# New order lists for the first eight steps of a fused attention and two-MoE kernel, with quotients, weight shifts, casts and low parts of g given out engine by engine

## The chip, the core and the metric

The kernel runs on one core of one Trainium2 chip. The metric is device microseconds of one launch. The kernel before has a median of 916.74 us over 3 runs (916.73 to 917.19).

## The reference

A banded attention feeds two feed-forward layers, all in fp32 to the reader; the weights come as 8-byte numbers.

```
scores = q k^T / 8, kept where 0 <= row - column < 64      4 batches, 8 heads, 576 rows, head size 64
x = softmax(scores) v                                      x: 2304 tokens x 512
g = x w_gate;  silu = g / (1 + exp(-g));  x = (silu * (x w_val)) w_out      inner size 1536
h = x w2_in;   out = max(0.01 h, h) w2_out                                  inner size 2048
```

## The kernel before, in words

The tokens are cut into five blocks. Block 0 holds 512 tokens and is worked in two halves of 256 (batch 0 and batch 1); blocks 1 to 4 hold 448 each. Per block the program first needs its attention, then the first layer in steps. One step takes 128 columns of the inner size: 12 matmuls for the gate (G), 12 for the value (W), 12 into the four output accumulators (O). Block 0 takes 24 steps, the others 12 each. The second layer follows, as products of halves in the manner of Strassen. Every matmul of the layers is done three times, with a high and a low part of both operands.

A weight piece of 128 x 512 comes in by a DMA (D) into one of three buffers `raw`. Five instructions make it ready: U on ScalarE scales the high word into `u` (L319), A shifts the low word right by 29 (L321), B joins the two (L323), C casts `u` to the high part (L330), E subtracts for the low part (L331). The buffer is free for the next DMA but two once B has read it. Each step has three pieces: g, v and o.

The attention of block 0 is eight jobs, 0 to 3 for the first half, 4 to 7 for the second, two heads each. A job n is: N, four transposes of q and k on TensorE; K, their eviction (L210); S, its scores; M and X, mask with row maximum and exponential, per tile t of 128 x 128; R, two small instructions for the reciprocals of the sums; Q, the quotient of a tile (L255); T, its transpose (L263); P, the eviction of T (L268); V, the values (L281); H and L, the high and low part of x (L291, L292). G of the first half needs H and L of jobs 0 to 3, quarter c of its matmuls those of job c. Per step also follow th, y (on G's result), z (on W's), gh and gl, the high and low part of the activation (L652, L654, L664, L666, L667). O needs gl.

Which instruction stands where on an engine comes from priorities, except at the start: `ORDER` names the instructions of the first steps engine by engine, and every instruction in such a list is tied behind the one before it. Each engine runs its own list strictly in order, so one that waits holds all behind it. In the kernel before all 32 quotients of block 0 are on GpSimd, all A on VectorE, all C on ScalarE and all gl on GpSimd; the lists end with G6, W6 and O5. Behind them the attention of block 1 (jobs 8 to 15) is laid into the remaining steps of block 0 by due times: job 8's are counted from slot 29, three slots to a step. Its q and k are turned by three transposes on VectorE (L214, L217).

Of the kernel before, what the change touches and what calls it, by code (L numbers as in the profile page):

```python
# [8 lines left out]
F32 = mybir.dt.float32  # L9
# [4 lines left out]
P = 128  # L14
# [13 lines left out]
def banded_attention_moe_moe(  # L28
# [99 lines left out]

    xt = {}
# [28 lines left out]
    class Job:  # L158


        def __init__(self, n, blk, xoff, b, u0, T, hp, first):
            self.n, self.blk, self.xoff, self.b, self.T, self.hp = n, blk, xoff, b, T, hp
            self.early = blk == 0
            self.half = u0 > 0
            self.N = 64 * T
# [77 lines left out]
        def norm(self, i, engines):  # L243
# [5 lines left out]
            for t, engine in zip(ts, engines):  # L249
                if engine is nc.scalar:  # L250
                    turn = nc.scalar.activation(e[:, t], e[:, t], AF.Copy, scale=st[:, 3, t:t + 1])
                elif engine is nc.vector:
# [4 lines left out]
                note(f"Q{self.n}.{t}", turn)  # L257

        def transpose(self, i):
            ts = self.fills[i]  # L260
            ps = (ps_acc if self.n < 4 else ps_att).tile([P, 4, P], F32, tag=self.bank, name="pt")
            for a, t in enumerate(ts):
                turned = note(f"T{self.n}", nc.tensor.transpose(ps[:, a], self.e[:, t], ident))  # L263
                if not self.early:
                    in_turn(turned)
            soon()
            note(f"P{self.n}",
                 nc.scalar.copy(self.pT[:, self.tile0 + ts[0]:self.tile0 + ts[-1] + 1], ps[:, :len(ts)]))  # L268
# [34 lines left out]
    def fetch(src, gated=False, key=None):  # L303
# [4 lines left out]
        note(key and "D" + key,  # L308
# [3 lines left out]
    def narrow(raw, gated=False, key=None):  # L312
# [16 lines left out]
    def split(hi, lo, u, key=None):  # L329
        note(key and "C" + key, nc.scalar.copy(hi, u))  # L330
        note(key and "E" + key, nc.vector.tensor_tensor(lo, u, f32(hi), op=ALU.subtract))  # L331

    def fetch1(f, c, gated=False):
        cs, cs2 = slice(f * P, f * P + P), slice(f * 2 * P, f * 2 * P + 2 * P)
        src = {"g": w_gate, "v": w_val, "o": w_out}[c]
        return fetch(src[cs, :] if c == "o" else src[:, cs2].rearrange("(c p) f -> p c f", p=P), gated, c + str(f))

    def convert1(f, c, raw, gated=False):
        u = narrow(raw, gated, c + str(f))
# [3 lines left out]
        split(w[:, 0], w[:, 1], u, c + str(f))  # L343
# [186 lines left out]
    for _ in range(8):  # L530
# [4 lines left out]
        (-0.61, "N0 N1 S0 S1 N3 N2 S3 S2 T0 T1 V0 T2 V1 T3 V2 V3 N6 N5"),  # L535
        (0.39, "N7 N4"),
        (2.39, "S7 S4"),
        (3.39, "S5 S6"),
        (5.39, "T7 T4"),
        (6.39, "V7 V4"),  # L540
        (7.39, "T5"),
        (8.39, "T6 V5"),
        (9.39, "V6"),
    )

    def early(part, j):
# [8 lines left out]
        elif part == "T":  # L555
            j.norm(0, [nc.gpsimd] * 4)
            j.transpose(0)
# [10 lines left out]

    for slot, parts in EARLY:
        for part in parts.split():  # L570
            at(slot, lambda part=part: early(part[0], jobs[int(part[1:])]))

    for n, j in enumerate(jobs):
# [67 lines left out]
    def step1(slot, blk, cols, f, first, last, behind=lambda *a: None, key=None):  # L641
# [25 lines left out]
        note(f"gl{key}", nc.gpsimd.tensor_tensor(g[1][:, :n], th, f32(g[0][:, :n]), op=ALU.subtract))  # L667
# [31 lines left out]
    for i, (part, f) in enumerate(order):  # L699
# [5 lines left out]
        for f1 in range(HELD, NF1):  # L705
# [7 lines left out]

    ORDER = {
        "tensor":
            "N0 N1 S0 S1 N3 N2 S3 S2 T0 T1 V0 T2 V1 T3 V2 V3 N6 N5 G0 N7 N4 W0 S7 S4 G1 S5 S6 W1 O0 T7 T4 G2 V7 "
            "V4 W2 T5 O1 T6 V5 G3 V6 W3 O2 G4 W4 O3 G5 W5 O4 G6 W6 O5",
        "vector":
# [5 lines left out]
        "scalar":  # L724
# [333 lines left out]
```

## Time and profile before

| | us |
|---|---|
| median of 3 runs | 916.74 |
| the profiled execution, its own time | 916.74 |
| its span, from the first to the last instruction | 914.9 |
| TensorE busy in the span | 900.2 |
| granted TensorE clock, mean | 0.998 |

The first slice of the profile's 40 shows TensorE at 7 tenths, the last at 8, all others at 9; so what TensorE leaves empty is to be looked for at the start and the end. VectorE is at 9 tenths in slices 2 and 5 of the start. The DMA engines' mean share is 9, 7, 6, 7 tenths in the first four slices.

### The profile page before, as it was taken

The page shows a single profiled execution, that of the slowest core. Times are in us where ns is not written, and L with a number is a line of the kernel's source. Part 1 is how long each engine was busy: PE and PEld are TensorE (multiplying, and loading weights), DVE is VectorE, ACT ScalarE, POOL GpSimd, SP SyncE. Part 2 cuts the span into 40 slices and gives each one's busy share as a digit, 9 for nine tenths or more (in the row PEclk, how much of TensorE's full clock was granted, in tenths as well). Part 3 has the DMA queues.
Part 4 walks back from the last instruction along what each step waited for, and adds up shares of the span by engine and source line. Part 5 has one row for each costly group of instructions (what it writes and reads, how often), then busy time and mean ns, then how long its engine had stood idle before and what let it go on. Part 6 is the DMA issues. An engine that isn't in the chain of part 4 may idle for free.

```text
span 914.9 us, 18179 instructions
## 1 busy us (share of the span) xinstructions
PE 900.2 (98%) x6147; PEld 855.6 (94%) x6147; DVE 661.3 (72%) x1525; ACT 462.3 (51%) x1153; POOL 374.3 (41%) x541
## 2 busy tenths in 40 slices
PE   7999999999999999999999999999999999999998
PEld 6899999899899999999999999999999999999997
DVE  5988974465666666566445546899998899978787
ACT  6956664554555545546433325544536445454442
POOL 4433321112212212212222135666666666675555
PEclk9999999999999999999999999999999999999999
DMA  9767642446576566746543966876568783588842
GB/s 232 214 176 201 189 119 48 114 152 200 163 207 170 170 177 189 210 144 212 171 178 136 338 208 208 266 236 222 176 196 286 243 255 114 164 281 264 247 152 81
DMA packets 198524, 176.32 MB, mean 193 GB/s; under 512 B 118048, under 2 KB 146976, under 8 KB 198432
## 3 DMA queue, kind: packets, MB, share of 16 engines
q1 hardware_dynamic: 196288, 174.64, 62.7%
q8 instruction: 49, 0.80, 0.4%
q10 hardware_dynamic: 2144, 0.52, 0.3%
q14 instruction: 43, 0.35, 0.1%
HBM read 135.27 MB, written 39.85 MB: 191 GB/s over the span
## 4 chain that ended last, share of the span: by engine, by line
PE 81%; DVE 7%; DMA 4%; POOL 2%; issue 2%; ACT 2%; SPq 1%; DVEq 0%; POOLq 0%; ACTq 0%
PE pv L610 14%; PE acc L610 14%; PE pg L610 14%; PE y L826 12%; PE px L783 7%; PE pw L783 5%; PE py L783 5%; PE yc L826 5%; PE s L227 2%; DMA raw<-in_moe_w_val_dram 2%; DVE space L820 2%; PE pv L281 1%; PE pt L263 1%; POOL g L805 1%; DVE u L323 1%
## 5 line engine op out<-in xcount | busy, mean ns | idle before, releaser
L667 POOL TENSOR_TENSOR g<-th,g 128x448 fp32r<-128x448 f32 (+1 forms) x72 | 82.0, 1138 | 265.0 <-ACT g L666 253.4
L610 PE MATMUL pv<-x,w 128*128 128x448 f32 (+1 forms) x864 | 172.0, 344 | 0.4 <-DVE w L331 0.2
L610 PE MATMUL pg<-x,w 128*128 128x448 f32 (+1 forms) x864 | 168.8, 342 | 1.7 <-DVE th L654 1.0
L610 PE MATMUL acc<-g,w 128*128 128x448 f32 (+1 forms) x864 | 166.0, 340 | 0.0
L610 PEld LDWEIGHTS acc<-g,w 128*128 128x128 f32 x864 | 144.4, 189 | 9.3 <-POOL g L667 0.3
L610 PEld LDWEIGHTS pg<-x,w 128*128 128x128 f32 x864 | 142.7, 189 | 10.8 <-DVE th L654 1.2
L610 PEld LDWEIGHTS pv<-x,w 128*128 128x128 f32 x864 | 142.2, 189 | 10.8 <-issue 0.7
L826 PE MATMUL y<-space,g 128*128 128x256 f32 x1035 | 145.7, 282 | 0.8 <-DVE space L820 0.5
L826 PEld LDWEIGHTS y<-space,g 128*128 128x128 f32 x1035 | 137.8, 190 | 1.8 <-DVE space L820 1.6
L820 DVE TENSOR_TENSOR space<-y,space 128x512 f32<-128x512 f32 (+1 forms) x180 | 102.0, 591 | 10.9 <-PE y L826 10.2
L805 POOL TENSOR_TENSOR g<-t,g 128x384 fp32r<-128x384 f32 x71 | 78.0, 1099 | 58.4 <-ACT g L804 47.9
L783 PE MATMUL px<-space,space 128*128 128x384 f32 x432 | 89.2, 337 | 0.0
L654 DVE SCALAR_TENSOR_TENSOR th<-th,pg 128x448 f32<-128x448 f32 (+1 forms) x72 | 39.5, 549 | 52.6 <-ACT th L652 52.2
L783 PEld LDWEIGHTS px<-space,space 128*128 128x128 f32 x432 | 74.2, 188 | 1.1 <-DVE t L1015 0.5
L666 ACT CAST g<-th 128x448 fp32r<-128x448 f32 (+1 forms) x72 | 36.9, 512 | 66.6 <-DVE th L664 66.5
L805 POOL TENSOR_TENSOR g<-c,g 128x384 fp32r<-128x384 f32 x47 | 50.1, 1066 | 39.3 <-ACT g L804 27.0
L826 PE MATMUL yc<-space,g 128*128 128x256 f32 x414 | 63.8, 282 | 0.0
L783 PE MATMUL py<-space,space 128*128 128x384 f32 x288 | 63.5, 336 | 0.0
L783 PE MATMUL pw<-space,space 128*128 128x384 f32 x288 | 62.8, 336 | 0.0
L319 ACT ACTIVATE u<-raw 128x512 f32<-128x512 f32 x68 | 45.4, 675 | 33.1 <-DMA raw<-in_moe_w_in_dram 15.3
L805 POOL TENSOR_TENSOR g<-u,g 128x384 fp32r<-128x384 f32 x47 | 56.0, 1198 | 9.2 <-ACT g L804 6.3
L240 ACT ACTIVATE e<-e,st 128x128 f32<-128x128 f32 x120 | 46.8, 391 | 23.0 <-DVE st L237 22.9
(142 smaller groups left out, 1458.0 us busy)
## 6 DMA issues: line engine op xcount, KB each, us to landing
space<-o SPq DMA_DIRECT2D x147, 256.0 KB, 3.4
space<-a SPq DMA_DIRECT2D x140, 256.0 KB, 3.8
raw<-in_moe_w_out_dram SPq DMA_DIRECT2D x28, 512.0 KB, 4.3
a<-hl SPq DMA_DIRECT2D x24, 512.0 KB, 2.8
o<-hl SPq DMA_DIRECT2D x24, 512.0 KB, 3.0
raw<-in_moe_w_in_dram SPq DMA_DIRECT2D x16, 512.0 KB, 4.8
raw<-in_moe_w_gate_dram SPq DMA_DIRECT2D x12, 512.0 KB, 4.1
raw<-in_moe_w_val_dram SPq DMA_DIRECT2D x12, 512.0 KB, 5.2
```

The source lines that it names most:

```text
L227: in_turn(nc.tensor.matmul(ps[:, a], lhsT=qbd[:, t, :], rhs=kT[:, w0:w0 + P], start=True, stop=True))
L240: nc.scalar.activation(e[:, t], e[:, t], AF.Exp, bias=st[:, 0, t:t + 1], scale=-1.0, accum_out=st[:, 1, t:t + 1]))
L263: turned = note(f"T{self.n}", nc.tensor.transpose(ps[:, a], self.e[:, t], ident))
L319: note(key and "U" + key, nc.scalar.activation(u, f32(high), AF.Prelu, scale=EXP_SCALE, alpha=NEGATIVE))
L610: note(key, nc.tensor.matmul(ps, lhsT=w(a, c), rhs=x(b, c), start=(start and n == 0), stop=(stop and n == 3 * len(cs) - 1), skip_group_che ...
L654: nc.vector.scalar_tensor_tensor(out=th, in0=th, scalar=1.0, in1=pg, op0=ALU.add, op1=ALU.mult))
L666: cast = note(f"gh{key}", nc.scalar.copy(g[0][:, :n], th))
L667: note(f"gl{key}", nc.gpsimd.tensor_tensor(g[1][:, :n], th, f32(g[0][:, :n]), op=ALU.subtract))
L783: nc.tensor.matmul(ps, lhsT=A2[n, k][:, a, c * P:c * P + P], rhs=X2[i, c, k][:, b], start=start and m == 0, stop=m == 5, skip_group_check= ...
L805: (lo or nc.gpsimd).tensor_tensor(g[:, 1], src, f32(g[:, 0]), op=ALU.subtract)
L820: nc.vector.tensor_tensor(f32(dst), ps, f32(dst), op=ALU.add)
L826: nc.tensor.matmul(ps, lhsT=g[:, a, r * P:r * P + P], rhs=O2[n, k][:, b], start=start and m == 0, stop=m == 2, skip_group_check=True)
```

## The change

The lists are written anew and reach to G7, W7 and O6. In them:

- the 32 quotients of block 0 are given out: 16 stay on GpSimd, 10 go to ScalarE, 6 to VectorE;
- 12 of the shifts A for f = 0 to 4 go to GpSimd, in another form: it reads byte 3 of the low word and computes byte/32 - 0.484375, rounded to a whole number, where VectorE shifts 32-bit words;
- casts C of v0, o1, v3 and o4 go to GpSimd; gl of steps 0, 4 and 6 goes to VectorE;
- the evictions change sides: K2, K3 and K7 on VectorE, K1, K5, K6 and K4 on ScalarE, P3 and P7 on VectorE;
- transposes T stand tile by tile, in the order in which the quotients are meant to come; G0 is cut into its four quarters, with V2, V3, N5 and N7 between them; the second half's jobs run 7, 6, 5, 4;
- block 1's jobs are counted from slot 26, and the transposes of job 8 may issue only behind z7.

```
-            "Q0.2 Q0.1 Q0.0 Q0.3 Q1.3 Q1.0 Q1.2 Q1.1 Q2.0 Q2.1 Q2.3 Q2.2 Q3.2 Q3.1 Q3.3 Q3.0 gl0 Q7.0 Q7.3 Q7.2 "
+            "Av0 Q1.2 Q1.3 Ao0 Q2.0 Q2.2 Q2.1 Q2.3 Q3.1 Cv0 Ag1 Ao1 Co1 Q7.0 Q7.3 Ag2 Av2 Q6.2 Ao2 Q6.0 Q6.1 Q5.3 "
+            "Q5.0 gl1 Q5.2 Ag3 Av3 Q4.1 Cv3 Ao3 gl2 Ag4 gl3 Ao4 Co4 gl5",
...
+    engine_of = {name: engine for engine, names in ORDER.items() for name in names.split()}
+    def engine_for(key, engine):
+        return getattr(nc, engine_of[key]) if key in engine_of else engine
+    def copy_on(engine):
+        return nc.scalar.copy if engine is nc.scalar else engine.tensor_copy
...
+        if engine_for(f"A{key}", nc.vector) is nc.vector:
+            shifted = nc.vector.tensor_single_scalar(part, low, 29, op=ALU.logical_shift_right)
+        else:
+            byte = raw.rearrange("p f two -> p (f two)").bitcast(mybir.dt.uint8).rearrange("p (f e) -> p f e", e=8)
+            shifted = nc.gpsimd.tensor_scalar(part, byte[:, :, 3], 0.03125, -0.484375, op0=ALU.mult, op1=ALU.add)
...
-        note(key and "C" + key, nc.scalar.copy(hi, u))
+        note(f"C{key}", copy_on(engine_for(f"C{key}", nc.scalar))(hi, u))
...
+    def first_quadrants(j):
+        with tc.issue_after(made["z7"][0]):
+            j.quadrants()
...
-        b0 = FIRST[j.blk - 1] + int(4.5 * i) + (29 if j.blk == 1 else -5)
+        b0 = FIRST[j.blk - 1] + int(4.5 * i) + (26 if j.blk == 1 else -5)
-        L(0, j.quadrants)
+        L(0, (lambda j=j: first_quadrants(j)) if n == 8 else j.quadrants)
```

GpSimd at the start, behind the masks. `e_94` holds the tiles of job 0, `nat` those of job 1, `rooms_97` of job 2, `rooms_96` of job 3 (then of jobs 7 and 6 in turn). The kernel before:

```order
L255 TENSOR_SCALAR e_94<-e_94,st 128x128 x4
L255 TENSOR_SCALAR nat<-nat,st 128x128 x4
L255 TENSOR_SCALAR rooms_97<-rooms_97,st 128x128 x4
L255 TENSOR_SCALAR rooms_96<-rooms_96,st 128x128 x4
L667 TENSOR_TENSOR g_505<-th,g_504 128x256
```

and the changed one:

```order
L377 TENSOR_SCALAR raw<-raw 128x512
L296 TENSOR_SCALAR nat<-nat,st 128x128 x2
L377 TENSOR_SCALAR raw<-raw 128x512
L296 TENSOR_SCALAR rooms_97<-rooms_97,st 128x128 x4
L296 TENSOR_SCALAR rooms_96<-rooms_96,st 128x128
L387 CAST w<-u 128x512
L377 TENSOR_SCALAR raw<-raw 128x512 x2
L387 CAST w<-u 128x512
```

Nine of the first sixteen quotients have left GpSimd; two shifts stand among the other seven, and behind them a cast, two shifts and a cast.

VectorE around the first transposes of block 1 (L214, L217). In the kernel before L654 and L664 below them are y6 and z6:

```order
L321 TENSOR_SCALAR raw<-raw 128x512
L331 TENSOR_TENSOR w<-u,w 128x512
L323 SCALAR_TENSOR_TENSOR u<-u,raw 128x512
L214 STREAM_TRANSPOSE kT<-inb 128x384
L217 STREAM_TRANSPOSE qbd<-inb 64x5x64
L331 TENSOR_TENSOR w<-u,w 128x512
L654 SCALAR_TENSOR_TENSOR th<-th,pg 128x256
L217 STREAM_TRANSPOSE qbd<-inb 64x5x64
L664 SCALAR_TENSOR_TENSOR th<-th,pv 128x256
```

In the changed one L715 and L725 above them are y7 and z7:

```order
L380 SCALAR_TENSOR_TENSOR u<-u,raw 128x512
L388 TENSOR_TENSOR w<-u,w 128x512
L715 SCALAR_TENSOR_TENSOR th<-th,pg 128x256
L373 TENSOR_SCALAR raw<-raw 128x512
L725 SCALAR_TENSOR_TENSOR th<-th,pv 128x256
L253 STREAM_TRANSPOSE kT<-inb 128x384
L256 STREAM_TRANSPOSE qbd<-inb 64x5x64 x2
L373 TENSOR_SCALAR raw<-raw 128x512
```

The transposes have moved from ahead of y6 to behind z7.

TensorE where block 1's first step begins (`pg` and `pv` of 128x448 are its G and W, of which nine matmuls each stand earlier; `acc` of 128x256 is block 0's last O; `pv` of 64 columns and of 64x128 the last values of block 1). Before:

```order
L610 MATMUL acc_642<-g_2349,w 128x256
L227 MATMUL s<-kT,qbd 128x128 x2
L281 MATMUL pv<-pT,inb 64x64 x10
L281 MATMUL pv<-pT,inb 64x128 x2
L610 MATMUL pg<-x,w 128x448
L610 MATMUL pv<-x,w 128x448
L610 MATMUL pg<-x,w 128x448 x2
L610 MATMUL pv<-x,w 128x448 x2
L263 MATMUL pt<-ident,e_94 128x128 x5
L227 MATMUL s<-kT,qbd 128x128 x2
L610 MATMUL pg<-x,w 128x448 x12
```

The change:

```order
L671 MATMUL acc_645<-g_2349,w 128x256
L332 MATMUL pv<-pT,inb 64x128 x2
L266 MATMUL s<-kT,qbd 128x128 x3
L671 MATMUL pg<-x,w 128x448
L671 MATMUL pv<-x,w 128x448
L266 MATMUL s<-kT,qbd 128x128 x2
L671 MATMUL pg<-x,w 128x448 x2
L671 MATMUL pv<-x,w 128x448 x2
L304 MATMUL pt<-ident,e_94 128x128
L671 MATMUL pg<-x,w 128x448 x12
```

Ten of the last twelve values stand eight matmuls earlier now, and scores stand between the last two and the gate, and between the first and the other two matmuls of the gate's last quarter.

## Rows read from the trace of the kernel before

**Rows 1.** The page: TensorE's busy time, share of the span, instructions.
```profile
PE 900.2 (98%) x6147; PEld 855.6 (94%) x6147; DVE 661.3 (72%) x1525; ACT 462.3 (51%) x1153; POOL 374.3 (41%) x541
```
**Rows 2.** Stretches: busy us (x instructions) by engine, granted TensorE clock, DMA share, GB/s.
```profile
12.00:16.00 4.00, 1.12 (x9) 0.56 (x5) 3.04 (x22) 3.18 (x16) 1.32 (x4) 1.00 0.86 188
16.00:20.00 4.00, 3.63 (x32) 2.85 (x31) 3.06 (x6) 3.71 (x10) 4.00 (x7) 0.57 1.21 237
30.00:40.00 10.00, 10.00 (x110) 9.34 (x108) 9.78 (x51) 9.64 (x40) 4.91 (x9) 1.00 0.59 188
160.00:200.00 40.00, 38.88 (x223) 34.99 (x224) 22.65 (x77) 21.00 (x64) 7.52 (x13) 1.00 0.45 116
300.00:500.00 200.00, 200.00 (x1196) 183.18 (x1196) 117.06 (x311) 98.16 (x254) 45.83 (x103) 1.00 0.58 179
```
**Rows 3.** TensorE's timeline, 12 to 36 us: start, us, instruction [idle before <- releaser].
```profile
15.68 0.33 PE L263 MATMUL pt<-ident,nat 128*128 128x128 f32 x1 [2.88 <-POOL nat L255]
...
17.19 0.69 PE L281 MATMUL pv<-pT,nat 128*64 128x128 f32 x4
...
21.07 0.66 PE L263 MATMUL pt<-ident,rooms 128*128 128x128 f32 x4 [0.86 <-POOL rooms L255]
...
24.11 1.09 PE L207 MATMUL qkt<-ident,nat 128*128 128x128 f32 x8 [0.98 <-DVE x L292]
...
30.77 1.69 PE L610 MATMUL pg<-x,w 128*128 128x256 f32 x12
```
**Rows 4.** GpSimd's timeline, 14 to 30 us.
```profile
14.68 1.64 POOL L255 TENSOR_SCALAR nat<-nat,st 128x128 f32<-128x128 f32 x4 [2.76 <-DVE st L248]
16.30 4.73 POOL L255 TENSOR_SCALAR rooms<-rooms,st 128x128 f32<-128x128 f32 x8
```
**Rows 5.** Timeline of ScalarE and VectorE, 9 to 40 us.
```profile
9.63 1.04 ACT L210 COPY rooms<-qkt 128x512 f32<-128x512 f32 x2
...
12.32 0.43 DVE L321 TENSOR_SCALAR raw<-raw 128x512 int32<-128x512 int32 x1 [0.97 <-DMA raw<-in_moe_w_val_dram]
...
39.89 0.40 DVE L321 TENSOR_SCALAR raw<-raw 128x512 int32<-128x512 int32 x1
```
**Rows 6.** Groups by form, 0 to 150 us: busy us, mean ns, idle before.
```profile
L330 ACT CAST w<-u 128x512 fp32r<-128x512 f32 x36 | 22.2, 618 | 7.9 <-DVE u L323 7.7
...
L210 DVE COPY rooms<-qkt 128x512 f32<-128x512 f32 x2 | 1.4, 686 | 2.3 <-PE qkt L207 2.3
```
**Rows 7.** One line's instructions, L255 up to 60 us: ns min/median/max.
```profile
L255 POOL TENSOR_SCALAR rooms<-rooms,st x16: 370/376/1318, 16.3 to 44.8; 128x128 f32<-128x128 f32 x16
```
**Rows 8.** GpSimd's groups by form, whole span.
```profile
L667 POOL TENSOR_TENSOR g<-th,g 128x448 fp32r<-128x448 f32 x48 | 61.0, 1271 | 198.8 <-ACT g L666 187.9 <-DMA inb<-in_v_dram 9.0 <-DVE ev L634 2.0
...
L667 POOL TENSOR_TENSOR g<-th,g 128x256 fp32r<-128x256 f32 x24 | 21.0, 874 | 66.1 <-ACT g L666 65.5 <-DMA inb<-in_q_dram 0.6
...
L255 POOL TENSOR_SCALAR e<-e,st 128x128 f32<-128x128 f32 x28 | 13.8, 508 | 16.3 <-ACT rooms L210 7.2 <-ACT g L666 6.2 <-DVE st L248 2.9
...
L126 POOL MEMSET qbd<- 128x640 f32 x1 | 0.6, 625 | 0.0
```
**Rows 9.** VectorE and GpSimd, timeline around 52 us.
```profile
52.40 1.28 DVE L331 TENSOR_TENSOR w<-u,w 128x512 fp32r<-128x512 f32 x2
52.46 2.17 POOL L667 TENSOR_TENSOR g<-th,g 128x256 fp32r<-128x256 f32 x1 [5.27 <-ACT g L666]
```
**Rows 10.** Timeline around 65 us.
```profile
64.08 0.58 DVE L214 STREAM_TRANSPOSE kT<-inb 128x384 f32<-128x384 f32 x1 [1.38 <-DMA inb<-in_k_dram]
...
65.55 0.40 DVE L654 SCALAR_TENSOR_TENSOR th<-th,pg 128x256 f32<-128x256 f32 x1
...
66.00 0.39 PE L610 MATMUL pg<-x,w 128*128 128x256 f32 x1 [0.95 <-DVE th L654]
```
**Rows 11.** TensorE's timeline, 158 to 164 us.
```profile
160.66 0.47 PE L610 MATMUL pg<-x,w 128*128 128x448 f32 x1 [0.75 <-ACT x L291]
...
163.70 0.71 PE L227 MATMUL s<-kT,qbd 128*128 128x128 f32 x4 [0.46 <-ACT pT L268]
```

More of the change, by code (lines that the diff above doesn't have):

```diff
@@ L164, in __init__ @@
             self.half = u0 > 0
+            self.turned = 0
             self.N = 64 * T
@@ L241, in scores, with norm @@
                                           accum_out=st[:, 1, t:t + 1]))
-        def norm(self, i, engines):
+        def norm(self, i, engine):
             soon()
@@ L256, in norm @@
                                                    op1=ALU.mult)
-                note(f"Q{self.n}.{t}", turn)
+                note(key, turn)
         def transpose(self, i):
@@ L262, in transpose, with turn @@
             for a, t in enumerate(ts):
-                turned = note(f"T{self.n}", nc.tensor.transpose(ps[:, a], self.e[:, t], ident))
-                if not self.early:
-                    in_turn(turned)
+                turned = nc.tensor.transpose(ps[:, a], self.e[:, t], ident)
+                in_turn(turned)
             soon()
-            note(f"P{self.n}",
-                 nc.scalar.copy(self.pT[:, self.tile0 + ts[0]:self.tile0 + ts[-1] + 1], ps[:, :len(ts)]))
+            nc.scalar.copy(self.pT[:, self.tile0 + ts[0]:self.tile0 + ts[-1] + 1], ps[:, :len(ts)])
+        def turn(self, t):
+            if not self.turned:
+                self.norm(0, nc.gpsimd)
+                self.ps = ps = (ps_acc if self.n < 4 else ps_att).tile([P, 4, P], F32, tag=self.bank, name="pt")
+            self.turned += 1
+            note(f"T{self.n}.{t}", nc.tensor.transpose(self.ps[:, t], self.e[:, t], ident))
+            if self.turned == 4:
+                soon()
+                key = f"P{self.n}"
+                note(key, copy_on(engine_for(key, nc.scalar))(self.pT[:, 0:4], self.ps))
         def values(self):
@@ L534, in banded_attention_moe_moe, with early @@
     EARLY = (
[L535 to L543, printed above, removed]
+        (-0.61, "N0 N1 S0 S1 N2 N3 S2 S3 T0.0 T0.1 T0.2 T1.0 T1.2 T1.3 T0.3 T2.0 T1.1 T2.2 V0 T2.1 T3.0 "
+                 "T2.3 V1 T3.1 T3.3 T3.2 V2 V3 N5 N7"),
+        (0.39, "N6 S7 S6"),
+        (3.39, "S5"),
+        (4.39, "T7.0 T7.1 T7.3 T7.2 N4 V7"),
+        (5.39, "S4 T6.0 T6.1 T6.3 T6.2"),
+        (6.39, "T5.0 T5.2 T5.3 T5.1 V6"),
+        (8.39, "V5 T4.0 T4.1 T4.3 T4.2"),
+        (9.39, "V4"),
     )
-    def early(part, j):
+    def early(part, j, t=None):
         if part == "N":
@@ L555, in early @@
         elif part == "T":
-            j.norm(0, [nc.gpsimd] * 4)
-            j.transpose(0)
+            j.turn(t)
         else:
@@ L567, in late_loads @@
                 j.load_v(True)
+    def first_quadrants(j):
+        with tc.issue_after(made["z7"][0]):
+            j.quadrants()
     for slot, parts in EARLY:
         for part in parts.split():
-            at(slot, lambda part=part: early(part[0], jobs[int(part[1:])]))
+            at(slot, lambda part=part: early(part[0], jobs[int(part[1])], *(int(t) for t in part[3:])))
     for n, j in enumerate(jobs):
@@ L711, in banded_attention_moe_moe @@
               lambda *a, i=i: convert_behind(i, *a), i)
[L714 to L718, printed above, removed]
[5 rows of a table removed]
-        "scalar":
[5 rows of a table removed]
-        "gpsimd":
-            "Q0.2 Q0.1 Q0.0 Q0.3 Q1.3 Q1.0 Q1.2 Q1.1 Q2.0 Q2.1 Q2.3 Q2.2 Q3.2 Q3.1 Q3.3 Q3.0 gl0 Q7.0 Q7.3 Q7.2 "
-            "Q7.1 Q4.3 Q4.0 Q4.1 Q4.2 gl1 Q5.2 Q5.3 Q5.0 Q5.1 Q6.2 Q6.0 Q6.3 Q6.1 gl2 gl3 gl4 gl5",
-        "sync":
-            "Dg0 Dv0 Do0 nv0a nv0b nv0c nat1a nat1b nat1c nat1d Dg1 Dv1 nv1a Do1 nv1b nv1c Dg2 Dv2 Do2 Dg3 Dv3 "
-            "Do3 Dg4 Dv4 Do4 Dg5 Dv5 Do5",
-    }
     for names in ORDER.values():
-        line = [i for name in names.split() for i in made[name]]
+        line = [i for name in names.split() for part in ([name] if name in made else [f"{name}.{a}" for a in range(4)])
+                for i in made[part]]
         for before, behind in zip(line, line[1:]):
```

47 lines of the change are left out of this document (30 added, 17 removed), and 24 rows, old and new, of the table ORDER.

## Prediction

> **What bounds the kernel now.** I read the page first: TensorE is busy 900.2 of the span's 914.9 us, VectorE 661.3, GpSimd 374.3 [rows 1]. Then stretches: from 300 to 500 us TensorE is busy all of 200.00 us, so a microsecond won earlier stays won to the end; the gaps are early. From 160 to 200 it is idle 1.12 us; from 30 to 40 it is full, and there VectorE and ScalarE are nearly so (9.78 and 9.64 of 10), GpSimd half (4.91); from 12 to 16 it is busy only 1.12 of 4 us, and from 16 to 20 its granted clock is 0.57, about the lower of its two levels (1.2 GHz) [rows 2]. So a rich place for a gain is 12 to 24 us, and the spare engine after it is GpSimd. TensorE's timeline names the gaps: 2.88 us before the second transpose group, 0.86 before job 3's, both released by GpSimd's quotients, then 0.98 behind the low part of x [rows 3]. GpSimd's timeline says why: job 1's quotients wait 2.76 us for VectorE's reciprocals, and then eight more stand in a row for 4.73 us [rows 4]. The reciprocals are late because ScalarE copies K3 and K2 (1.04 us) ahead of job 1's exponentials, and because VectorE stands 0.97 us at the shift of v0, which waits for its DMA [rows 5]. Two later gaps: 0.95 us before G7, which waits for y6 (65.55), itself behind job 8's transposes, which wait 1.38 us for the DMA of k [rows 10]; and 0.75 + 0.46 us where block 1 begins [rows 11].
>
> The profiled execution took 916.74 us, which is also the median; 1.84 us of it lie outside the span. I count from 916.74.
>
> **The start.** K2 and K3 go to VectorE: two copies of 0.686 us [rows 6] against 1.04 saved on ScalarE, so job 1's exponentials end about 11.2 instead of 12.2. The shift of v0 goes to GpSimd and waits there for its DMA, landing 12.3; VectorE no longer stands behind it, but Q1.2 and Q1.3 do.
>
> GpSimd's shift (128x512, a byte in, a whole number out) is in no row. From below: its memset of 640 columns takes 0.625 us [rows 8], so about 0.6. From above: four times a quotient of 128 columns, 4 x 0.508 = 2.0 [rows 8]. Between: going from 256 to 448 columns its low part of g grows from 874 to 1271 ns, 2.07 ns a column; added to the fastest quotient, 370 ns [rows 7], 384 columns more give 1.16. I take 1.2, the value worked out from a slope, and 1.1 for a cast. On VectorE the shift costs 0.43 [rows 5], on ScalarE the cast 0.618 [rows 6]: the work grows, only the engine changes.
>
> With these, GpSimd runs Av0 12.3 to 13.5, Q1.2 and Q1.3 to 14.5, Ao0 to 15.7, Q2.0 and Q2.2 to 16.7; ScalarE's Q1.1 ends about 16.1 and P0 16.6. The first values start at 17.0, where they stood at 17.19 [rows 3]: almost nothing yet, and since TensorE again waits from 12 to 16, I leave its clock as it was. But jobs 2 and 3 no longer need eight quotients in a row: four more are on VectorE, and job 2's are half done. The second values start about 18.3, job 3's transposes end 19.3 (21.73: 21.07 + 0.66 [rows 3]). G0's first quarter goes at 19.5, V2 20.0, V3 20.8, G0's second quarter 21.5, and with N5, N7, N6, S7, S6 and W0 (27.0) between, G1 at 28.5. Before it was 30.77 [rows 3]; ahead of it the new list lacks only N4, half of 1.09 us [rows 3]. **Lead: 30.77 - 28.5 - 0.55 = 1.7 us.**
>
> **From 24 to 60 us** the lead must be kept. VectorE loses eight shifts for f = 1 to 3, 8 x 0.43 = 3.4 us, and gets two evictions of 0.7 (K7, P7) and the low part of step 0; where it is busy 9.78 of 10 us that is room. GpSimd gets, from G0's place (24.1 [rows 3]) to where Ag3 stood on VectorE (39.89 [rows 5]) and 1.2 more, six shifts, one cast, eight quotients, one low part: 7.2 + 1.1 + 8 x 0.5 + 0.8 = 13.1 us of 17.0. There is room, so I cost it at nothing; with shifts and cast of 2.0 it is 14 + 4 + 0.8 = 18.8, and the cover is gone. A wait is added: Co1 stands behind o1's joining (B) on VectorE and holds Q7.0, Q7.3 and Ag2 behind it; T7 needs them only behind W1. P7 on VectorE, behind M5, holds V7 back by about half an eviction, 0.35 us (N4 covers the rest), and I allow 0.15, which no row gives, for more switches between attention and layer work. **Given back: 0.5. Lead at step 6: 1.2.**
>
> One thing speaks against all this. A low part of g took 2.17 us while two E, VectorE's two-input subtractions, ran beside it for 1.28 [rows 9]; its mean is 0.874 [rows 8]. The Trainium skill, "SBUF — State Buffer", section "Who interferes with whom", has a rule for it: VectorE and GpSimd share one pair of ports, whoever starts first holds it for its whole instruction, and the other blocks fully. The trace agrees in this instance: 2.17 - 0.874 = 1.30, the two E. By that rule a shift that meets a B or an E waits it out, 1.2 + 0.64 = 1.84 us, an estimate, and the sum would lie near the slower rival's below; by the rows alone, with 1.2, it does not.
>
> **Job 8's transposes** now stand behind z7. k lands at 64.08 [rows 10] and z7 will be about 66.5, so nothing waits there, and y6 no longer stands behind them. What stands behind them now is the shift and joining of v6, with a step to spare. **0.95 gained.** If the landings come later with the new order, up to as much again is lost at Av6.
>
> **The stage boundary.** Block 1's jobs come three slots (one step) sooner, and scores now lie between the last values and the gate and between the gate's matmuls. Four scores take 0.71 us from start to end [rows 11]; three now run while x is made, and cover 0.35 of the 0.75 (they overlap, so less than 3 x 0.18). The 0.46 ends with ScalarE's P, which frees the bank of those scores; they need it as before, only earlier, so I take about half, 0.25. **0.6 gained**, with bounds of 0 and 1.1 (all that is idle there).
>
> **Sum:** 916.74 - 1.2 - 0.95 - 0.6 = **914.0 us**.
>
> **The rivals.**
> Weights' chain (rival B): each piece needs one of three buffers and a landing; from 12 to 20 us the mean DMA share is already 0.86 to 1.21 [rows 2], so TensorE, early at W1 or O1, waits there instead. Against it: GpSimd's shifts free buffers sooner, if they are not slower than VectorE's queue was. The lead goes; 0.95 + 0.6 stay: 915.2.
>
> GpSimd becomes the bound (rival C), on the slower side: a shift beside VectorE's two-input work takes 2.0 us. The 18.8 us above then overrun their 17.0 by 1.8, and a queue behind each DMA holds quotients, so Q1.2 and Q2.2 come 0.8 and 1.6 late at the start (the lead of 1.7 is gone), and the second half's quotients hold T6, T5 and T4 and with them V6, V5 and V4, behind which W2, O1 and W3 stand: the overrun of 1.8, and three DMAs that start later by as much in turn (v2, o2, v3: 0.6 each, by an even share), some 3.5 us late at step 6, less 0.95 and 0.6: 916.74 + 3.5 - 1.55 = 918.7. It decides from a shift of about 1.7 us on, where lead and delay cancel. For it: rows 9. Against it: quotients in the same busy stretch have a median of 376 ns though the longest took 1318 [rows 7].
>
> Cheap shifts (rival D): 0.7 to 0.9 us each, near the memset's 0.625. The quotients of jobs 1 and 2 come 0.3 to 0.8 sooner, half of it behind P0 anyway: 1.9 of lead are left at step 6, and 916.74 - 1.9 - 1.55 = 913.3.
>
> Block 1's part does not do what it says (rival E): job 8's transposes only hand their wait on to the joining of v6, and at the boundary x is late whatever stands before it. The lead alone remains: 915.5.
>
> **How the numbers follow.** Forecast 0.44 (its own range 912.8 to 914.9), B 0.23, C 0.18, D 0.10, E 0.05. Under 0.2%, 1.83 us, a measurement of this kernel can't tell a change from none: faster means under 914.9, slower over 918.6. Faster: 0.40 of the forecast, 0.10 of D, 0.03 of B = 0.53. Slower: 0.13 of C, whose tail is long (the cast and low parts slow too). The rest, 0.34, is the same. The range takes in D and most of C: 912.3 to 918.2; outside lie about 0.05 below and 0.12 above.
>
> **What would show it.** Right: the gap of 2.88 stays near as long in sum but is cut up, the one of 0.86 is gone, V3 starts near 20.8 and G1 near 28.5; GpSimd's shifts have a mean of about 1.2; G7 has no gap; from 160 to 200 us TensorE is idle under 0.6. Wrong: shifts with a mean over 1.7, TensorE's gaps between 30 and 50 us released by quotients (C), or released by DMAs of `raw` or by B (B); TensorE waiting for a piece behind Av6, the boundary's two gaps still 1.2 together (E).

## The result, and the profile after

The changed kernel takes 923.01 us (median of 6; 921.0 to 925.69) where the kernel before takes 916.46 (median of 6): a ratio of 1.0077 [1.0063, 1.0091], the brackets giving a 95% interval. It is slower, clear of noise; 914.0 was forecast and 918.2 was the upper end. The ratios in this document are the measured ones with their intervals; they differ by up to 0.08% from the quotients of the medians, which here is 1.0071. The profiled execution took 923.15 us with a span of 921.4, so its gain and loss can be counted against the 914.9 of before: 6.5 us.

I read three stretches of the trace after. The first is the start. TensorE's timeline, which answers to [rows 3]:

```profile
13.99 0.52 PE L315 MATMUL pt<-ident,nat 128*128 128x128 f32 x3 [1.35 <-DVE nat L294]
...
16.32 0.49 PE L332 MATMUL pv<-pT,nat 128*64 128x128 f32 x4
...
18.05 0.70 PE L332 MATMUL pv<-inb,nat 128*64 128x128 f32 x4
...
28.27 1.60 PE L671 MATMUL pg<-x,w 128*128 128x256 f32 x12
```

The gap of 2.88 us is cut up (1.35 is its largest piece), the first values start at 16.32 and G1 at 28.27, where it was 30.77. GpSimd's groups by form, 0 to 60 us (busy us, mean ns, idle before), price the two operations that no row of before showed:

```profile
L377 POOL TENSOR_SCALAR raw<-raw 128x512 int32<-128x512 uint8 x12 | 9.8, 815 | 18.8 <-DMA raw<-in_moe_w_val_dram 8.9 <-DMA raw<-in_moe_w_gate_dram 3.9 <-DVE w L388 2.9
...
L387 POOL CAST w<-u 128x512 fp32r<-128x512 f32 x4 | 3.0, 745 | 4.5 <-DVE u L380 4.5
```

A shift takes 0.815 us on average, a cast 0.745. The second stretch is the moved job. VectorE's timeline around z7:

```profile
66.04 0.41 DVE L715 SCALAR_TENSOR_TENSOR th<-th,pg 128x256 f32<-128x256 f32 x1
69.25 0.43 DVE L373 TENSOR_SCALAR raw<-raw 128x512 int32<-128x512 int32 x1 [2.80 <-DMA raw<-in_moe_w_gate_dram]
69.59 0.41 DVE L725 SCALAR_TENSOR_TENSOR th<-th,pv 128x256 f32<-128x256 f32 x1
69.95 0.58 DVE L253 STREAM_TRANSPOSE kT<-inb 128x384 f32<-128x384 f32 x1
```

Job 8's transposes indeed wait for nothing. But between y7 (66.04) and z7 (69.59) stands the shift of g6, which waits 2.80 us for its DMA. TensorE waits for z7 in turn (1.29 us, ahead of W8), and goes on waiting for VectorE in the steps behind it:

```profile
67.17 1.60 PE L671 MATMUL pg<-x,w 128*128 128x256 f32 x12
70.06 1.70 PE L671 MATMUL pv<-x,w 128*128 128x256 f32 x12 [1.29 <-DVE th L725]
...
91.62 0.62 PE L671 MATMUL pv<-x,w 128*128 128x256 f32 x3 [0.65 <-DVE th L725]
...
97.74 1.67 PE L671 MATMUL pv<-x,w 128*128 128x256 f32 x12 [1.10 <-DVE th L725]
```

The DMA queue's own timeline says where the weight stands: behind block 1's first loads, which issue from 56.88 to 64.9.

```profile
56.88 1.96 SPq L224 DMA_DIRECT2D inb<-in_k_dram  x4
58.89 3.88 SPq L224 DMA_DIRECT2D inb<-in_q_dram  x4
62.87 2.02 SPq L238 DMA_DIRECT2D inb<-in_v_dram  x4
64.99 0.38 SPq L360 DMA_DIRECT2D raw<-in_moe_w_gate_dram  x1
```

It stood behind them in before too, and was issued at 65.94 there: the weight is 0.95 us sooner, while TensorE is over 3 us sooner. How long the wait is differs between executions. The experiment o_behind_values (below) runs the same order up to block 0's last O and has TensorE at the same place at this time, but its four issues of q took 2.04 us where the change's took 3.88; its shift waited 0.41 us, and W8 did not wait at all:

```profile
58.81 2.04 SPq L224 DMA_DIRECT2D inb<-in_q_dram  x4
```

```profile
66.98 0.43 DVE L373 TENSOR_SCALAR raw<-raw 128x512 int32<-128x512 int32 x1 [0.41 <-DMA raw<-in_moe_w_gate_dram]
```

The third stretch is the stage boundary, where before had waits of 0.75 and 0.46 [rows 11]:

```profile
160.33 1.21 PE L671 MATMUL acc<-g,w 128*128 128x256 f32 x8
161.47 0.44 PE L332 MATMUL pv<-pT,inb 128*64 128x128 f32 x4
161.84 0.94 PE L266 MATMUL s<-kT,qbd 128*128 128x128 f32 x6
...
164.66 0.68 PE L266 MATMUL s<-kT,qbd 128*128 128x128 f32 x4 [1.31 <-DVE x L343]
...
167.47 0.47 PE L304 MATMUL pt<-ident,e 128*128 128x128 f32 x1 [1.32 <-ACT e L292]
167.60 4.83 PE L671 MATMUL pg<-x,w 128*128 128x448 f32 x12
```

Two waits of 1.31 and 1.32 us stand there now, and the next twelve gate matmuls take 4.83 us. Stretches of TensorE by windows (columns as in [rows 2]) show that its clock had fallen:

```profile
160.00:170.00 10.00, 7.36 (x48) 5.89 (x45) 5.51 (x22) 6.31 (x21) 1.13 (x1) 0.84 0.60 143
170.00:180.00 10.00, 10.00 (x46) 9.04 (x45) 2.98 (x9) 2.64 (x8) 1.16 (x2) 0.82 0.11 37
```

For a running account I take, in each trace, the start of the first matmul of each group of twelve O's, and subtract the start in before (O0 35.81, O6 68.98, O22 150.94, O34 255.28). Minus is a lead. Each row is one profiled execution, and the fastest and the slowest execution of one kernel lie 0.2 to 0.8% apart. How much a single trace can say is seen in two places. Fourteen of the traces run the same instructions in the same order up to O5; there they stand between 2.44 us ahead and 1.49 behind, with a median of 1.87 ahead. And the change and o_behind_values have the same order up to block 0's last O, yet stand at +2.38 and 0.00 at O22. So the ratios carry the argument, and the account only says where to look.

| kernel | O0 | O6 | O22 | O34 | ratio to before [95%] |
|---|---|---|---|---|---|
| the change | -1.35 | -3.25 | +2.38 | +7.06 | 1.0077 [1.0063, 1.0091] |
| block1_back | -1.04 | -1.48 | -1.36 | -1.46 | 0.9973 [0.9962, 0.9983] |
| slot29_held | -1.27 | -3.48 | -0.32 | -0.77 | 0.9985 [0.9974, 0.9996] |
| slot29_behind_z6 | -0.52 | -2.29 | -0.37 | -0.70 | 0.9969 [0.9956, 0.9981] |
| slot26_free | -1.55 | -2.82 | -0.13 | -0.07 | 1.0004 [0.9992, 1.0016] |
| o_behind_values | -1.59 | -3.36 | 0.00 | -0.44 | 1.0022 [1.0010, 1.0033] |
| quotients_on_gpsimd | -0.06 | +0.68 | +0.78 | +0.46 | 1.0012 [1.0003, 1.0021] |

The change has a lead of 3.25 us at O6. It loses 5.63 up to O22 and 4.68 from there to O34, and nothing afterwards (0.56 of it comes back by the end).

### The profile page after: what moved, and what is told of

It is laid out like the page before. It is cut to its first block, busy times and chain, and to the rows that moved or that the text cites. A ratio compares the mean times of both kernels' runs of the same rounds, so it can differ in the third digit from the quotient of the medians.

```text
span 921.4 us, 18199 instructions
## 1 busy us (share of the span) xinstructions
PE 905.4 (98%) x6147; PEld 858.6 (93%) x6147; DVE 660.6 (72%) x1524; ACT 463.3 (50%) x1157; POOL 377.9 (41%) x538
## 5 line engine op out<-in xcount | busy, mean ns | idle before, releaser
L729 POOL TENSOR_TENSOR g<-th,g 128x448 fp32r<-128x448 f32 (+1 forms) x69 | 78.1, 1133 | 250.5 <-ACT g L727 240.4
L671 PE MATMUL pg<-x,w 128*128 128x448 f32 (+1 forms) x864 | 173.1, 346 | 0.6 <-DVE th L715 0.5
L671 PE MATMUL acc<-g,w 128*128 128x448 f32 (+1 forms) x864 | 168.0, 341 | 0.0
L671 PEld LDWEIGHTS pg<-x,w 128*128 128x128 f32 x864 | 144.7, 191 | 9.8 <-DVE th L715 0.9
L715 DVE SCALAR_TENSOR_TENSOR th<-th,pg 128x448 f32<-128x448 f32 (+1 forms) x72 | 39.6, 550 | 55.0 <-ACT th L713 54.6
L352 POOL CAST hl<-g 128x1 fp32r<-128x1 f32 x66 | 17.4, 270 | 105.2 <-DMA a<-hl 46.3
```

Of the source, the lines that this page charges most:

```text
L352: nc.gpsimd.tensor_copy(tile, mark[0])
L715: nc.vector.scalar_tensor_tensor(out=th, in0=th, scalar=1.0, in1=pg, op0=ALU.add, op1=ALU.mult))
L729: engine_for(f"gl{key}", nc.gpsimd).tensor_tensor(g[1][:, :n], th, f32(g[0][:, :n]), op=ALU.subtract))
```

## The experiments

**Which part costs.** The first four part the start's edits from block 1's. The start's edits alone, with block 1 as before:

```
-        b0 = FIRST[j.blk - 1] + int(4.5 * i) + (26 if j.blk == 1 else -5)
+        b0 = FIRST[j.blk - 1] + int(4.5 * i) + (29 if j.blk == 1 else -5)
...
-        L(0, (lambda j=j: first_quadrants(j)) if n == 8 else j.quadrants)
+        L(0, j.quadrants)
```

> The changed kernel with block 1's jobs counted from slot 29 again and job 8's transposes free to issue where they fall, the new lists kept. Theory (block 1's jobs one step sooner put their loads of q and k ahead of weight loads on SyncE's queue, shifts then wait for a DMA between y and z, and the stage boundary goes wrong): the lead of 2.0 us at O5 stays, no wait of over 1 us on VectorE's z from 84 to 120 us, boundary gaps about 1.2 us together and no fall of the clock; only z7 behind the shift of g6 still costs about 1.3: 915.5 to 916.5 us. Rival (the lists of the start cost it, with shifts and casts on GpSimd): 921 to 923 us as the changed kernel.

Measured 913.04 us, 0.9973, better than the theory's range. So the start's edits gain 0.27%, and block 1's part costs the difference to 1.0077, 1.04% or 9.5 us. Its trace keeps its lead (table). The same slot in the kernel before, and nothing else:

```
-        b0 = FIRST[j.blk - 1] + int(4.5 * i) + (29 if j.blk == 1 else -5)
+        b0 = FIRST[j.blk - 1] + int(4.5 * i) + (26 if j.blk == 1 else -5)
```

> The kernel before with block 1's jobs counted from slot 26, nothing else; its lists end with O5. Theory (the slot count is the cost): slower by 2 to 5 us, 918.5 to 921.5, with waits on VectorE's y or z from 84 to 120 us and larger gaps at the stage boundary. Rival (the slot count alone is harmless, it hurts only with the new lists): 916 to 917 us.

1.0017 [1.0004, 1.0029], 917.0 us, the upper end of the rival's range: an earlier block 1 costs there too, but a sixth of it. Then z7 ahead of the waiting shift, with the change and with block 1 put back:

```
-            "... y7 Ag6 z7 Av6 Bg6",
+            "... y7 z7 Ag6 Av6 Bg6",
```

> The changed kernel with z7 ahead of the shift of g6 in VectorE's list, nothing else. Theory: W8 loses its wait of 1.29 us, the later waits (0.65 and 1.10 near 91 and 97 us, the boundary, the clock) stay: 921.0 to 922.5 us. Rival (z7 behind that shift starts the whole loss): under 918 us.

> Both edits together: block 1's jobs from slot 29, transposes free, z7 ahead of the shift of g6. Theory: the lead of 2.0 us is kept to the end, 914.3 to 915.3 us. Rival (the start's lists cost more than they give later on): 917 us or more.

1.0022 [1.0009, 1.0036] and 0.9986 [0.9972, 1.0000]. The first, 917.34 us, is the rival's number and 0.55% better than the change, and its W8 no longer waits. But its order at the stage boundary has turned too: all of block 0's last O now stands behind the last values, where in the change the last four of their records come behind it.

```profile
160.76 0.44 PE L332 MATMUL pv<-pT,inb 128*64 128x128 f32 x4
...
163.73 1.36 PE L671 MATMUL acc<-g,w 128*128 128x256 f32 x10
```

Its account shows no loss there (+4.92 at O22, +4.86 at O34). It was already behind, at +1.49, by O5, in an execution whose granted clock was 0.87, 0.93 and 0.94 in the first three stretches of 20 us, where the change has 0.91, 1.00 and 1.00. So the gain can't be credited to the place of the shift: the boundary's order by itself is worth as much (o_behind_values, below), and where block 1 stands as before, z7 first gains nothing.

**Slot and hold apart.** One edit of block 1's two at a time: only 26 to 29, or only the hold of job 8 removed.

> The changed kernel with block 1's jobs counted from slot 29, job 8's transposes still held behind z7. Theory (the slot count is the cost, the hold is harmless): 912.0 to 914.0 us, as with both edits undone (913.04) or up to 1 us better, since y6 no longer stands behind the transposes. Rival (the hold behind z7 sets off the waits that follow): over 916 us, with waits of TensorE on VectorE's y or z after 80 us.

> The changed kernel with job 8's transposes free to issue where they fall, block 1's jobs still from slot 26. Theory (the slot count is the cost): 917 to 923 us, waits of TensorE on VectorE's y or z between 84 and 125 us of at least 2 us together. Rival (the hold is the cost): 913 to 914.5 us.

0.9985 (913.77 us, in the theory's range) and 1.0004 (915.29, in neither range). Against block1_back the hold alone costs 0.12% (intervals overlap) and the slot alone 0.31%; together they cost 1.04%, more than their sum of 0.43%. Where each loses in its trace is in the windows 62 to 70 and 70 to 118 us, idle TensorE being the stretch less its busy time. The change:

```profile
62.00:70.00 8.00, 6.77 (x57) 6.57 (x55) 4.12 (x11) 2.56 (x5) 0.38 (x2) 1.00 0.80 213
70.00:118.00 48.00, 45.16 (x379) 43.42 (x380) 41.09 (x116) 30.54 (x81) 16.95 (x33) 1.00 0.67 189
```

block1_back:

```profile
62.00:70.00 8.00, 6.73 (x54) 6.32 (x53) 6.02 (x14) 2.77 (x6) 0.39 (x3) 1.00 0.84 217
70.00:118.00 48.00, 48.00 (x419) 47.60 (x419) 43.20 (x119) 33.72 (x90) 20.11 (x36) 1.00 0.68 194
```

slot29_held:

```profile
62.00:70.00 8.00, 7.50 (x63) 7.29 (x62) 5.11 (x13) 2.97 (x6) 0.79 (x3) 1.00 0.82 241
70.00:118.00 48.00, 45.92 (x397) 44.97 (x395) 42.44 (x115) 31.51 (x86) 18.68 (x34) 1.00 0.67 187
```

The change is idle 1.23 + 2.84 us there, block1_back 1.27 + 0.00, slot29_held 0.50 + 2.08: the hold takes the gap away before 70 and it is back, larger, after. In slot29_held VectorE's shift of g6 waits too:

```profile
68.24 0.43 DVE L373 TENSOR_SCALAR raw<-raw 128x512 int32<-128x512 int32 x1 [1.79 <-DMA raw<-in_moe_w_gate_dram]
```

In this trace the step ahead is simply sooner than its weights. The loads three slots sooner at slot 29, without the hold (all loads share one buffer here, so a job's transposes read the next job's q and k: this kernel computes something else with the same sizes and counts, and only its time is read):

```
-        L(0, nxt.load)
+        L(-3 if j.blk == 1 else 0, nxt.load)
```

> The changed kernel with block 1's jobs from slot 29 and transposes free, but the loads of q and k of its jobs 9 to 15 issued three slots sooner, where slot 26 would have them. Theory A (these loads ahead of the weight loads on SyncE's queue make the shifts late): 1 to 3 us slower than without (913.04): 914 to 916 us, with shifts on VectorE waiting for DMAs of raw. Theory B (VectorE's own queue, with scores' masks and transposes of block 1 between y and z, is the cost, the loads are not): 912.5 to 913.6 us.

0.9989 [0.9979, 1.0000]. The 914.39 us lie in theory A's range, but the interval overlaps that of block1_back (0.9973 [0.9962, 0.9983]), so that the loads cost anything is not shown.

**The start's edits.** All twelve shifts back on VectorE (slot 29, no hold), each ahead of its joining B; and, apart from it, all 32 quotients back on GpSimd with the shifts and casts left there:

```
         "vector":
+            "... Av0 Bv0 ... Ao0 Bo0 ... Ag1 Bg1 ...
         "gpsimd":
-            "Av0 Q1.2 Q1.3 Ao0 Q2.0 ...
+            "Q1.2 Q1.3 Q2.0 ...
```

```
         "gpsimd":
-            "Av0 Q1.2 Q1.3 Ao0 Q2.0 Q2.2 Q2.1 Q2.3 Q3.1 Cv0 Ag1 ...
+            "Q0.0 Q0.1 Q0.2 Q0.3 Av0 Q1.2 Q1.3 Q1.0 Q1.1 Ao0 Q2.0 ...
```

> The changed kernel with block 1 as in the kernel before (slot 29, transposes free), and the 12 shifts back on VectorE, each right ahead of its joining. Theory (the lead of the start rests on the shifts leaving VectorE): the lead at O5 falls from 1.5 to 0.5 us or less, 914 to 915.5 us. Rival (on shared ports a shift on GpSimd costs VectorE as much as it saves; the lead comes from the quotients and evictions alone): 912.5 to 913.5 us.

> The new lists with slot 29 and transposes free, all 32 quotients back on GpSimd in about the old order, shifts and casts staying there too. Theory (the quotients' row was the gate of the start, and GpSimd now has the shifts besides): the second values and job 3's transposes come 2 us or more later, no lead at O0 or a delay up to 2 us, 915 to 918 us. Rival (quotients are cheap there, the lead came from the evictions and the shifts): lead at O0 of 0.7 us or more, under 914 us.

1.0003 [0.9994, 1.0012] and 1.0012 [1.0003, 1.0021]: either undone takes the gain of 0.27% away. The account at O5 stands at 0.00 us in the one and +0.78 in the other, where block1_back has -1.55 and the fourteen traces have a median of -1.87. With all quotients on GpSimd TensorE waits for it again at the first transposes:

```profile
15.17 0.55 PE L316 MATMUL pt<-ident,nat 128*128 128x128 f32 x3 [2.34 <-POOL nat L297]
```

**Is it the loads ahead of the weights?** My theory then was that an earlier block 1 costs because its loads stand ahead of the weights. In the change, and in slot26_free, the loads of jobs 10 to 15 come three slots later, tied behind the last weight load made:

```
-        L(0, nxt.load)
+        L(3 if j.blk == 1 and n > 8 else 0, (lambda nxt=nxt: load_behind(nxt)) if j.blk == 1 and n > 8 else nxt.load)
...
+    def load_behind(j):
+        last = [made[f"D{c}{f}"][0] for f in range(NF1) for c in "gvo" if f"D{c}{f}" in made][-1]
+        with tc.issue_after(last):
+            j.load()
```

> The changed kernel with the loads of q and k of block 1's jobs 10 to 15 put behind the weight loads on SyncE's queue that they stood behind in the kernel before (three slots later in the program, and each tied behind the last weight load then issued); jobs still from slot 26, job 8 held behind z7. Theory A (the loads ahead of the weight loads cost most): the loss from O6 to O22, 5.6 us in the profile, falls under 3, 917 to 919.5 us. Theory B (VectorE's own queue, with masks and transposes between y and z, costs it): 921 to 923 us.

> The same queue order with job 8's transposes free; without the edit this took 915.29 us, 1.0004 of the kernel before. Theory A: ratio 0.997 to 0.999, near slot 29's 0.9973, and the wait of 1.59 us for y near 93 us gone. Theory B: 1.000 to 1.002, the wait for y still there.

1.0059 [1.0041, 1.0077] and 1.0041 [1.0025, 1.0057]. The loss from O6 to O22 is 6.81 us in the first, where the change has 5.63, and 3.20 in the second, where slot26_free has 2.69; and the second still waits 1.60 us for y, near 94 us. So the theory falls. That the second is 0.37% worse than slot26_free can't be put down to the loads alone, since its order at the boundary has turned as well (see below). The hold moved a step sooner, behind z6, at slot 29 and at slot 26:

```
-        with tc.issue_after(made["z7"][0]):
+        with tc.issue_after(made["z6"][0]):
```

> The changed kernel with block 1's jobs from slot 29 and job 8's transposes held behind z6 instead of z7. Theory (free, they hold y6 back by 1.0 us; behind z7 they stand behind the shift of g6, which waits for a DMA, and the weights of step 9 stand behind them; behind z6 neither): 0.4 to 1.2 us better than free, ratio 0.996 to 0.997. Rival (k's DMA hands its wait on wherever they stand): ratio 0.9973 to 0.9985.

> The changed kernel with the hold at z6 instead of z7 and nothing else: slot 26 stays. Theory (late transposes of job 8 push every job of block 1 behind it, since one buffer takes the loads of all; with z6 they are not late): the stage boundary is whole, ratio 0.999 to 1.001 as with free transposes (1.0004). Rival (any hold at slot 26 is bad): over 1.003.

0.9969 [0.9956, 0.9981], in the theory's range, and 1.0034 [1.0018, 1.0050], the rival's. The first, 913.22 us, is ahead of both kernels (as block1_back is, which it can't be told from). At slot 26 even this hold costs 0.3% against none, and the boundary shows the waits of the change:

```profile
162.90 0.68 PE L266 MATMUL s<-kT,qbd 128*128 128x128 f32 x4 [1.31 <-DVE x L343]
...
165.71 0.46 PE L304 MATMUL pt<-ident,e 128*128 128x128 f32 x1 [1.32 <-ACT e L292]
165.82 4.22 PE L671 MATMUL pg<-x,w 128*128 128x448 f32 x12
```

**The boundary by itself.** In the change, block 0's last twelve O may issue only behind block 1's last values. The order up to there is the change's, instruction for instruction:

```
+        vs = [made[f"V{m}"][-1] for m in range(16) if f"V{m}" in made]
+        with tc.issue_after(vs[-1]) if last and blk == 0 else contextlib.nullcontext():
             for c in range(KC):
                 mm3(acc[c][:, cols], ...
```

> The changed kernel with one tie more: block 0's last twelve O matmuls stand behind the last values of block 1 that precede them in the program. The instruction order is the changed kernel's up to the stage boundary; there the last values and three scores now stand ahead of O, and on VectorE the low part of x and the masks ahead of the evictions. Theory (at the boundary O and its evictions hold the last attention, TensorE waits 1.3 us twice, and its clock then falls): 3 to 4.5 us faster than the changed kernel's 923.0, ratio to the kernel before 1.003 to 1.005, no fall of the clock near 166 us. Rival (the late attention of block 1, not the order at the boundary, makes TensorE wait): under 1 us, ratio 1.0065 or more.

1.0022 [1.0010, 1.0033], a little better than the theory's range: this one tie gives back 0.55% of the 1.04. Its trace (timeline, then windows) has the twelve O in one piece, one wait in place of two, and a full clock:

```profile
158.47 1.68 PE L671 MATMUL acc<-g,w 128*128 128x256 f32 x12
...
163.14 2.70 PE L671 MATMUL pg<-x,w 128*128 128x448 f32 x12 [1.34 <-DVE th L718]
```

```profile
160.00:170.00 10.00, 8.66 (x48) 7.62 (x47) 5.07 (x20) 6.78 (x23) 1.16 (x1) 1.00 0.62 160
170.00:180.00 10.00, 10.00 (x54) 9.26 (x53) 3.28 (x11) 2.69 (x8) 2.83 (x6) 1.00 0.09 15
```

Its account goes from 0.00 to -0.44 where the change's goes from +2.38 to +7.06. Its profiled execution was its fastest (914.48), so the size is taken from the medians. What is left, 1.0022 less 0.9973 or 0.49%, is about the sum of slot and hold (0.43%).

The other traces fit this. Of the nine with block 1 at slot 26, four have the change's order at the boundary and its two waits of 1.3 us (the change, after_loads_behind, slot26_behind_z6 and slot26_free_loads_behind); from O22 to O34 they lose 4.68, 1.55, 3.37 and 1.54 us. Five have the last O behind the values and one wait of 1.14 or 1.34 us there (before_slot26, slot26_free, z7_first, slot26_job10_behind_y12 and o_behind_values); they lose 0.06 us at most. Only o_behind_values names the boundary; elsewhere its order turned with a hold, with later loads or with the place of z7. That is why slot and hold cost more together than one by one.

**What is left at slot 26.** In slot26_free VectorE makes job 10's transposes ahead of y12, and TensorE waits 1.59 us for it:

```profile
90.89 0.57 DVE L253 STREAM_TRANSPOSE kT<-inb 128x384 f32<-128x384 f32 x1
...
91.96 1.03 DVE L256 STREAM_TRANSPOSE qbd<-inb 64x320 f32<-64x320 f32 x2
...
93.10 0.41 DVE L715 SCALAR_TENSOR_TENSOR th<-th,pg 128x256 f32<-128x256 f32 x1
```

```profile
93.57 1.70 PE L671 MATMUL pg<-x,w 128*128 128x256 f32 x12 [1.59 <-DVE th L715]
```

So job 10's transposes behind y12, and, against "the later the better", block 1 at slot 31 without the hold:

```
+        with tc.issue_after(made["y12"][0]):
+            j.quadrants()
```

```
-        b0 = FIRST[j.blk - 1] + int(4.5 * i) + (26 if j.blk == 1 else -5)
+        b0 = FIRST[j.blk - 1] + int(4.5 * i) + (31 if j.blk == 1 else -5)
```

> Block 1's jobs from slot 26, transposes of job 8 free, and those of job 10 tied behind y12, which they stood ahead of (TensorE then waited 1.59 us for y12 near 93.6 us; the kernel without the tie took 1.0004 of the kernel before). Theory (VectorE's own queue of masks and transposes ahead of y is what slot 26 costs there): that wait falls under 0.5 us and the ratio to 0.998 to 0.9995. Rival (the late weights hold y12's successors anyway): ratio 1.000 or more, with the wait in another place.

> The new lists with block 1's jobs counted from slot 31, transposes of job 8 free (26: 1.0004 of the kernel before; 29: 0.9973). Theory (until about 120 us the weights fill VectorE; every step sooner puts more of block 1's masks, transposes and reciprocals into that stretch): as good as 29 or better, 0.996 to 0.9975. Rival (the slot only decides the order by chance, or the boundary comes too early for the last job): 0.999 or more.

1.0030 [1.0017, 1.0044] and 1.0009 [0.9997, 1.0020], both the rival's figure. The wait at y12 is gone and the time is 0.26% worse, with waits elsewhere; slot 31 is 0.36% worse than slot 29. Its trace has a wait of the same kind:

```profile
104.00 1.70 PE L671 MATMUL pg<-x,w 128*128 128x256 f32 x12 [1.21 <-DVE th L715]
```

## Why the prediction was wrong

**The start: right, and larger.** The steps came where they were put: first values 16.32 (17.0 said), second 18.05 (18.3), G1 28.27 (28.5). At G1 that is 30.77 - 28.27 - 0.55 = 1.95 of lead for 1.7. At the O of step 5 it is 2.04 for 1.2 (1.87 as the median of the fourteen traces). The mis-sized terms are the shift (0.815, not 1.2) and the cast (0.745, not 1.1): the cheap-shift rival's condition held, with its 1.9 of lead. Both halves of the edit are needed for it, as the two experiments on shifts and quotients show.

**G7's 0.95: it came, and was no gain.** From O5 to O6 the lead grows from 2.04 to 3.25. The step that failed is "What stands behind them now is the shift and joining of v6, with a step to spare", and with it the sum, which carries the lead from there to the boundary as if nothing could cost it: the change lost 5.63 us from O6 to O22. Two things were missed. The list, shown with the change, has the shift of g6 between y7 and z7 (in before z7 went first); I had looked at what stands behind the transposes, not at what stands ahead of them.

```profile
69.19 0.42 DVE L664 SCALAR_TENSOR_TENSOR th<-th,pv 128x256 f32<-128x256 f32 x1
...
70.23 0.43 DVE L321 TENSOR_SCALAR raw<-raw 128x512 int32<-128x512 int32 x1
```

And nothing said that the weights, and VectorE with them, come sooner because TensorE does: at slot 29 with the hold, 3.48 us of lead at O6 are 0.32 at O22, and every kernel with the new start whose ratio is under 1 is between 0.3 and 1.8 us ahead at O22. The second seems the larger part: o_behind_values, without a wait at W8, still falls from 3.36 us of lead at O6 to none at O22, with a wait of 1.08 us for z near 95 us where the change has its 1.10. That is the rival of the weights' chain, right in kind, though put at W1 and not at step 7. The prediction's own escape, "up to as much again is lost at Av6", was too small and at the wrong shift.

**The boundary's 0.6: wrong in sign.** Bounds of 0 and 1.1 came from the idle time that was there [rows 11], as if an earlier job could only fill it. I read the order at this place and counted the scores that now cover x, and those too short: the trace shows each of these matmuls as two records, so the 0.71 us were two scores, and the three that cover x take 0.94, not 0.35. I did not ask what else was behind: the last two values (four records, from 161.47) follow block 0's last O, and VectorE does that O's evictions, and the next job's last transposes and two masks, ahead of the low part of x, which starts 2 us behind the values:

```profile
160.87 1.29 DVE L695 COPY ev<-acc 128x512 f32<-128x512 f32 x2 [5.54 <-PE acc L671]
...
163.89 0.62 DVE L343 TENSOR_TENSOR x<-pv,x 128x448 fp32r<-128x448 f32 x1
```

VectorE's idle time of 5.54 us ahead of the evictions is not the cost, for it idles 5.06 us at this place in before too; but there its evictions start at 158.76, ahead of those values (158.90). The waits of 1.31 and 1.32 us come from there, and the lower clock, where it came, followed them. o_behind_values shows it: with the values ahead of the O the pattern and 0.55% of the time are gone, and in its trace the clock does not fall.

**The rivals.** None had block 1's part as a cost; the last of them only had it do nothing. The slower side was given to GpSimd's shifts alone. With the start right and the sum of block 1's part -9.5 us where +1.55 was counted, that is the whole error.

**What stays open.** Why slot 26 costs 0.31% without the hold is not settled. Of two causes tried, the loads' place and job 10's transposes, each made it worse when undone, and slot 31 costs as well. Nor is it known why a hold or later loads turn the order at the boundary. All these edits but o_behind_values also move the order of everything behind them, so none is a clean subtraction. That the transposes and low parts on VectorE take turns with y and z in steps whose weights have just come is read from the waits, not shown. How the 0.55% parts between the waits and the clock is known for single executions alone: from O22 to O34 the change lost 4.68 us, 3.4 of them by the clock (below), and after_loads_behind, with the same waits at full clock, 1.55 (+3.15 to +4.70), as slot26_free_loads_behind 1.54. How often the clock falls in the executions that were only timed is not known.

## What to carry to other kernels

Moving a job sooner fills a gap only if everything that its engine queue holds between the job and its next reader is sooner too: list both neighbours of the moved piece, and ask which of them waits for a DMA that nobody has moved. A lead at one place is not a gain until the next transfer that does not follow it; price it where the stretch is full, not where it was won. And where a stage ends, the bound of an edit is not the idle time that is there: a job that slips behind the last work of the old stage can cost several times as much, so it needs a rival on the slower side of its own. Before single edits are added up or subtracted, compare the order of instructions at the places that they do not name: here a boundary that turned unasked was worth more than the edits.

## What the runs showed of the hardware

Two short waits can cost more than their length. Behind waits of 1.31 and 1.32 us, with 1.5 us of matmuls between them, the change's granted clock is 0.84 from 160 to 170 us and 0.82 from 170 to 180: 1.6 and 1.8 of 10 us lost, half of some 6.8 us at the lower level (1.2 GHz). Twelve gate matmuls take 4.83 us there; in o_behind_values, at 1.00, they take 2.70. In slot26_behind_z6 the same waits are followed by 4.22 us for these twelve. Of all eighteen traces these two alone show a granted clock under 1.00 between 60 and 200 us, in windows of 10 and 20 us. In after_loads_behind and slot26_free_loads_behind the same pattern is followed by no fall, so these waits don't always bring it:

```profile
165.42 0.68 PE L266 MATMUL s<-kT,qbd 128*128 128x128 f32 x4 [1.32 <-DVE x L343]
...
168.23 0.33 PE L304 MATMUL pt<-ident,e 128*128 128x128 f32 x1 [1.32 <-ACT e L292]
168.32 2.68 PE L676 MATMUL pg<-x,w 128*128 128x448 f32 x12
```

GpSimd's shift takes 0.652 us at least and 1.172 at most, a median of 0.676 over twelve. The longest ran beside two E, VectorE's two-input subtractions:

```profile
44.96 1.73 DVE L388 TENSOR_TENSOR w<-u,w 128x512 fp32r<-128x512 f32 x2
45.00 1.17 POOL L377 TENSOR_SCALAR raw<-raw 128x512 int32<-128x512 uint8 x1
```

Two E take 1.28 us in [rows 9] and 1.73 here, so each side lost about half a microsecond (0.45 and 0.50). The rule of the Trainium skill that the prediction weighed ("SBUF — State Buffer", section "Who interferes with whom") agrees with that if the shift waited out the rest of one E and the next E waited for the shift. The estimate made from it, 1.84 us for a shift, was too high as a mean: over the twelve shifts the mean lies 0.815 - 0.676 = 0.14 us above the median. That such meetings are the cause of the other long ones is not shown.
